# Four feature tiles share two passes of 64 + 64 inner rows in a feed-forward product, with other rules for the list scheduler

## The chip, the cores and the metric

One core of one Trainium2 chip runs the kernel. TensorE (PE) multiplies, VectorE (DVE) and ScalarE (ACT) do element work, GpSimd (POOL) and SyncE (SP) mostly issue transfers. The metric is the device time of one execution in microseconds (us). A weight load of PE (PEld) and a matmul are separate instructions of one engine.

## The reference

Two layers, each a windowed attention and a feed-forward part, over 2048 rows of 576 columns, all float32:

```python
    x = x + _A_ref(_layernorm(x, axis=-1), A_wqkv, A_wo)
    x = x + _B_ref(_layernorm(x, axis=-1), B_w1, B_w2)
    x = x + _A_ref(_layernorm(x, axis=-1), A_wqkv, A_wo)
    x = x + _B_ref(_layernorm(x, axis=-1), B_w1, B_w2)
```

`_A_ref` has 32 heads of 18 columns; a row attends to itself and the 7 rows that lie 2, 4, ... 14 before it. `_B_ref` is `silu(x @ w1) @ w2` with `w1` 576 x 4608 and `w2` 4608 x 576.

## The kernel before

**Tiling.** The rows are cut into four chunks of 512 (four tiles of 128 rows, index j). A stage s = 0 to 7 is one chunk of one layer: `front(s)` does attention, output projection and the layer norm ahead of the feed-forward part, `ffn(s)` the feed-forward part. The 4608 features are 36 tiles of 128, index f.

**Precision.** A float32 operand is split into a float16 high half and a float16 rest, the low half; a product is the sum of high x high, high x low and low x high. The inner dimension of 576 is four blocks of 128 and one of 64. Each full block takes three passes of a 128x128 weight tile against 512 columns. The block of 64 stands twice in the 128 partitions (high half of x in one, low half in the other), so that one pass gives two of its three parts; the third part (high x against the low half of the weights) needs only 64 partitions. So a feature tile takes 13 full passes and half a pass (`passes` yields 14; the last is the half one). `mm` issues the 13 passes of tile f, and `mm_both` the two half passes of the tiles f and f + 1: one on partitions 0 to 63, one on 64 to 127, into the two `z` banks. For this the transposed x (`xb`) carries a tenth section, which holds the block of 64 on the upper partitions.

**Down product.** `mm2` multiplies the activated tiles `h` with `w2` into `acc` (groups of 6 features in stage 0, of 9 later), `add_to` adds them to x. ACT applies silu (`hs <- z`) and makes the high half of `h`; DVE makes its low half.

**First chunk.** In stage 0 the weights come as float32 (`raw_load`, on POOL's queue), are scaled and split (`raw_split`: squares and high halves on ACT, low halves on DVE, L814 and L819) and are stored to DRAM for stages 1 to 7. In the same stretch DVE computes the attention of stage 1. PE also projects chunks 1 to 3 ahead of their attention (`qkv_ahead`).

**The order.** Every piece of work is an `op` with an engine, an assumed duration, a priority and what it reads and writes. `Plan.order` is a list scheduler: it simulates the engines with the assumed durations and issues, for each engine that is free, the ready op of the best priority whose buffers are free. What it returns is the fixed order of the program; each engine then works its own list in that order and waits for what is missing. The buffers matter here: `z` (2 PSUM banks), `misc` (2 banks, used by the projections and small sums), `acc` (2 x 2 banks), `h` (9), `hs` (3), `w1` (6), `w2` (11), `kv` (2).

**Transposes.** `transposed` turns the split layer norm with PE (`on_pe`) or with transposing DMAs on SP's queue.

Of the kernel before, what the change touches and what calls it, by code (L numbers as in the profile page):

```python
# [16 lines left out]
P = 128  # L17
# [7 lines left out]
NC = 4  # L25
NJ = 4
# [24 lines left out]
class Plan:  # L51
# [3 lines left out]
    LAT = 0.2  # L55
    DMA_IN, DMA_OUT = 1.2, 1.8
    DMA_RATE = 0.33e6

# [43 lines left out]
    def order(self):  # L102
        free = {t: list(range(len(x))) for t, x in self.tags.items()}
# [3 lines left out]
        ready = {e: [] for e in engines}  # L107
        events, out, tbl = [], [], None
        queues = {e: [] for e in engines}
# [57 lines left out]
        while done < len(self.ops):  # L167
# [12 lines left out]
            for e in engines:  # L180
# [7 lines left out]
                while ready[e]:  # L188
                    x = heapq.heappop(ready[e])
                    need = [b for b in x[2].bufs if b.slot is None]  # L190
                    n = {}
                    for b in need:
                        n[b.tag] = n.get(b.tag, 0) + 1
                    if all(len(free[t]) - want.get(t, 0) >= c for t, c in n.items()) and all(
                            self.turns[b.tag] in (None, b.turn) for b in need):
                        o = x[2]
                        break
                    for t, c in n.items():
                        want[t] = want.get(t, 0) + c
                    back.append(x)  # L200
# [11 lines left out]
                if e == "ACT" and o.table and o.table != tbl:  # L212
                    tbl = o.table
                    dur += 1.3
                o.start = now
                busy[e] = now + dur
# [15 lines left out]
def sliding_attention_silu_ffn(ctx: ExitStack, tc: tile.TileContext, x, wqkv, wo, w1, w2, out):  # L232
# [15 lines left out]
    def T(b):  # L248
        return S.tags[b.tag][b.slot]
# [24 lines left out]
    tag("acc", 2, [P, 2, 512], F32, ps, turns=False)  # L274
    tag("misc", 2, [P, 512], F32, ps, turns=False)

    xd = [[tc.dram_tile([P, D], F32, name=f"xd{c}{j}") for j in range(NJ)] for c in range(NC)]
# [55 lines left out]
    def passes(xk, wk):  # L333
# [6 lines left out]
        yield xk(4), wk(9)  # L340

    def halves_lo(src, f, s):
        for o, a, b in ((640, 0, 512), (D, 512, D)):
            nc.vector.scalar_tensor_tensor(f[:, o:o + b - a], src[:, a:b], s, f[:, a:b],  # L344
                                           op0=ALU.mult, op1=ALU.subtract)
# [24 lines left out]

    PE_LN = (1, 1, 1, 0)
    PACE_WQ, PACE_WO, PACE_W = (1, 7, 0, 6), (2, 2, 3, 3, 3), (4, 5, 6, 7)
# [231 lines left out]
    def attention(s, xT, wq, more=None):  # L604
# [4 lines left out]
        for u in range(NU):  # L609
# [11 lines left out]
            else:  # L621
# [13 lines left out]
                for j in range(NJ):  # L635
                    m = Buf("misc")

                    def evac(j=j, m=m, u=u, kv=kv, qt=qt):
                        d = du[:, u:u + 1]
                        nc.scalar.activation(T(kv)[:, j + W - 1].rearrange("p a b -> p (a b)"), T(m)[:, UC:3 * UC],  # L640
                                             AF.Copy, scale=d)
                        nc.scalar.activation(T(qt)[:, j, :], T(m)[:, 0:UC], AF.Copy, scale=d)
                    op("PE", 2.6, lambda j=j, m=m, w=w: qkv_matmul(xT, w, j, m),
                       [(xT, j)] + w.keys, [m], pr_)
                    op("ACT", 0.9, evac, [m, ("su", u)], [(kv, j), (qt, j)], pr_ - (0 if s else 9))
# [194 lines left out]
    def ffn(s, xT, xs):  # L840
# [3 lines left out]
        lay, c = divmod(s, NC)  # L844
        pair = {}
        for g in range(NFT // n):
# [8 lines left out]
            for f in range(g * n, (g + 1) * n):  # L855
                if f % 2 == 0:

                    for q in (f, f + 1):
                        wab = ws[q - g * n] if raw else (load_w1(q, pd), load_w2(q, pd))
                        pair[q] = (Buf("z"), *wab, *([[(w, 0), (w, 1)] for w in wab] if raw else [[w] for w in wab]))  # L860
                z, wa, wb, ka, kb = pair[f]
                hs, h = Buf("hs"), Buf("h")
                hb.append(h)
                wbs.append((wb, kb))

                def mm(z=z, wa=wa, f=f):
                    pl = list(passes(lambda k: T(xT)[:, k, :], lambda k: T(wa)[:, k, :]))[:-1]
                    for m, (u, v) in enumerate(pl):
                        nc.tensor.matmul(T(z), v, u, start=m == 0 and f % 2 == 0, stop=m == len(pl) - 1 and f % 2 == 1)  # L869

                def mm_both(f=f):
                    for q, p0, k in ((f, 0, 4), (f + 1, 64, 9)):
                        nc.tensor.matmul(T(pair[q][0]), T(pair[q][1])[p0:p0 + 64, 9, :], T(xT)[p0:p0 + 64, k, :],  # L873
                                         start=q != f, stop=q == f)
                xk = [(xT, j) for j in range(NJ)]
                op("PE", 2.81, mm, xk + ka, [z], pp)
                if f % 2 == 0:
                    op("PE", 0.3, mm_both, xk + ka + pair[f + 1][3], [z, pair[f + 1][0]], pp)
                op("ACT", 0.7, lambda z=z, hs=hs, f=f: nc.scalar.activation(T(hs), T(z), AF.Silu, scale=d1[:, f:f + 1]),  # L879
# [70 lines left out]
    def front(s):  # L950
# [22 lines left out]
        project(s, o, X[s])  # L973
        XT[s] = layer_norm(X[s], s - 1.0, "xb", s == 1, s == 0, True)

# [35 lines left out]
```

## Time and profile before

| what | value |
|---|---|
| median of 3 runs | 2227.76 us (2226.75 to 2228.0) |
| the profiled execution | 2227.76 us; span from first to last instruction 2226.0 us |
| PE busy | 2180.7 us (98%) |
| DVE busy | 1394.7 us (63%) |
| ACT busy | 758.1 us (34%) |
| mean granted clock of PE | 0.998 of 2.4 GHz |

The profiled execution's own time is its span plus 1.8 us around it, and is the median itself. Matmuls are pipelined: a matmul of 512 columns is listed with 380 ns, but the next one starts sooner, so what PE gets done is read from the starts of its instructions and not from their durations.

### The profile page before, as it was taken

The numbers are of one execution on the slowest core, as the hardware profiler recorded it, in microseconds if no ns is written. First come the engines' busy times: TensorE is split into PE (matmuls) and PEld (weight loads), VectorE is DVE, ScalarE is ACT, GpSimd is POOL, SyncE is SP. The second block draws the span as 40 slices with busy tenths as digits, with TensorE's granted clock in tenths as the row PEclk, the third lists the DMA queues.
The fourth block names the chain that finished last, engine by engine and source line by source line (L and its number), as shares of the span: only waits on it lengthen the run. The fifth ranks groups of instructions, "written<-read, shape, count | busy, mean of one in ns | idle before, by whom it ended". The sixth has DMA issues, their size and how long they took to land.

```text
span 2226.0 us, 33948 instructions
## 1 busy us (share of the span) xinstructions
PE 2180.7 (98%) x13862; PEld 1325.1 (60%) x13862; DVE 1394.7 (63%) x2047; ACT 758.1 (34%) x1219; POOL 205.1 (9%) x341
## 2 busy tenths in 40 slices
PE   5999999999999999999999999999999999999999
PEld 3556465656666666655666656656566566666665
DVE  7899989998988411249843598336873378621111
ACT  6456666643133122224212242222322223222222
POOL 2123454400001000000000000000000000000000
PEclk9999999999999999999999999999999999999999
DMA  5578666874555433445445454454445453353331
GB/s 162 155 203 277 229 230 208 258 214 158 145 186 161 113 107 103 149 128 176 115 119 157 131 151 122 126 159 140 130 116 136 149 162 114 70 140 121 114 111 42
DMA packets 225045, 333.11 MB, mean 150 GB/s; under 512 B 111720, under 2 KB 132052, under 8 KB 220920
## 3 DMA queue, kind: packets, MB, share of 16 engines
q1 hardware_dynamic: 195888, 231.39, 36.0%
q0 software_dynamic: 20704, 78.02, 10.4%
q10 hardware_dynamic: 8296, 21.52, 3.5%
q8 instruction: 108, 1.77, 0.3%
q14 instruction: 49, 0.40, 0.1%
HBM read 240.08 MB, written 47.03 MB: 129 GB/s over the span
## 4 chain that ended last, share of the span: by engine, by line
PE 90%; DMA 3%; DVE 3%; ACT 1%; issue 1%; POOL 1%; SPq 0%; ACTq 0%; DVEq 0%; POOLq 0%
PE acc L898 36%; PE z L869 34%; PE misc L573 9%; PE acc L743 4%; PE z L573 4%; PE z L873 2%; DMA w<-in_B_w_dram 1%; DMA h<-in_A_wqkv_dram 1%; DVE w L814 0%; DMA x<-in_A_x_dram 0%; DMA kv<-kd 0%; DVE pr L704 0%; DVE yh L344 0%; DMA kd<-hs 0%; DVE x L750 0%
## 5 line engine op out<-in xcount | busy, mean ns | idle before, releaser
L898 PE MATMUL acc<-w,h 128*128 128x288 f16 x6912 | 859.7, 286 | 2.3 <-DVE h L884 1.6
L869 PE MATMUL z<-xb,w 128*128 128x512 f16 x3744 | 841.5, 380 | 6.5 <-DVE w L814 6.3
L898 PEld LDWEIGHTS <-h 128*128 128x128 f16 x6912 | 675.7, 98 | 181.7 <-issue 4.0
L869 PEld LDWEIGHTS <-w 128*128 128x128 f16 x3744 | 355.7, 98 | 441.7 <-issue 31.4
L879 ACT ACTIVATE hs<-z,d 128x512 f32<-128x512 f32 x288 | 197.7, 686 | 1001.8 <-PE z L873 511.1
L884 DVE SCALAR_TENSOR_TENSOR h<-hs,sh,h 128x512 f16<-128x512 f32 x288 | 214.6, 749 | 391.0 <-ACT h L881 390.8
L750 DVE SCALAR_TENSOR_TENSOR x<-acc,d,x 128x576 f32<-128x576 f32 x135 | 110.1, 816 | 301.7 <-PE acc L898 301.6
L881 ACT ACTIVATE h<-hs,sh 128x512 f16<-128x512 f32 x288 | 207.4, 721 | 9.1
L573 PEld LDWEIGHTS <-xa 128*128 128x128 f16 x1344 | 131.9, 98 | 121.3 <-issue 7.2
L573 PE MATMUL misc<-wq,xa 128*128 128x432 f16 x1008 | 190.1, 349 | 3.6 <-ACT xa L360 2.5
L671 DVE TENSOR_TENSOR pr<-qt,kv 128x2304 f32<-128x2304 f32 x64 | 163.4, 2553 | 13.6 <-DMA kv<-kv 12.7
L704 DVE TENSOR_TENSOR pr<-kv,pe 128x1152 f32<-128x1152 f32 x128 | 169.2, 1352 | 1.1
L675 DVE TENSOR_REDUCE lg<-pr 128x128 f32<-128x2304 f32 x64 | 163.1, 2549 | 1.2
L711 DVE TENSOR_TENSOR pr<-pr 128x1152 f32<-128x1152 f32 (+1 forms) x128 | 135.3, 1057 | 3.6
L743 PE MATMUL acc<-wo,oT 128*128 128x288 f16 x896 | 113.5, 286 | 0.0
L743 PEld LDWEIGHTS <-oT 128*128 128x128 f16 x896 | 87.6, 98 | 22.7
L640 ACT ACTIVATE kv<-misc,du 128x288 f32<-128x288 f32 x80 | 40.0, 500 | 145.3 <-PE misc L573 98.1
L922 POOL DMA_DIRECT2D out_dram<-x x12 | 6.5, 544 | 685.6 <-DVE x L750 685.6
L573 PEld LDWEIGHTS <-xb 128*128 128x128 f16 x448 | 43.6, 98 | 39.1 <-ACT xb L360 1.9
L873 PE MATMUL z<-xb,w 64*128 64x512 f16 x288 | 57.3, 386 | 2.8 <-DMA x<-in_A_x_dram 2.6
L750 DVE SCALAR_TENSOR_TENSOR x<-acc,so,x 128x576 f32<-128x576 f32 x32 | 26.1, 816 | 48.1 <-PE acc L743 48.0
L390 DVE BATCH_NORM_STATS2 st<-x 128x6 f32<-128x288 f32 x128 | 51.8, 447 | 6.0 <-DMA x<-in_A_x_dram 4.8
(123 smaller groups left out, 1165.2 us busy)
## 6 DMA issues: line engine op xcount, KB each, us to landing
w<-w1s SPq DMA_DIRECT2D x252, 320.0 KB
w<-w2s SPq DMA_DIRECT2D x252, 288.0 KB
wq<-wqs SPq DMA_DIRECT2D x17, 1080.0 KB
kv<-kd POOLq DMA_DIRECT2D x8, 1584.0 KB, 8.6
w1s<-w POOLq DMA_DIRECT2D x36, 320.0 KB, 4.1
w<-in_B_w_dram POOLq DMA_DIRECT2D x36, 288.0 KB, 4.4
w2s<-w POOLq DMA_DIRECT2D x36, 288.0 KB, 4.0
kv<-kv ACTq DMA_DIRECT2D x20, 504.0 KB
```

Source lines behind the costliest of these rows:

```text
L573: nc.tensor.matmul(T(m)[:, :3 * UC], a, b, start=n == 0, stop=n == len(pl) - 1)
L671: nc.vector.tensor_tensor(T(pr), T(qt)[:, j:j + 2, None, :].to_broadcast([P, 2, W, UC]), win(T(kv), j, 2), op=ALU.mult)
L675: nc.vector.tensor_reduce(T(lg)[:, j:j + 2].rearrange("p a w h -> p (a w h)"), T(pr).rearrange("p a w (h d) -> p (a w h) d", d=DH), axis=A ...
L704: nc.vector.tensor_tensor(T(pr)[:, a].rearrange("p w (h d) -> p w h d", d=DH), v, T(pe)[:, j + a, :, :, None].to_broadcast([P, W, UH, DH]) ...
L711: nc.vector.tensor_tensor(t[:, :, 0:h, :], t[:, :, 0:h, :], t[:, :, h:2 * h, :], op=ALU.add)
L743: nc.tensor.matmul(T(acc)[:, h, 0:288], a, b[:, h * 288:(h + 1) * 288], start=n == 0, stop=n == len(pl) - 1)
L750: nc.vector.scalar_tensor_tensor(t, T(acc)[:, :, 0:288], d, t, op0=ALU.mult, op1=ALU.add)
L869: nc.tensor.matmul(T(z), v, u, start=m == 0 and f % 2 == 0, stop=m == len(pl) - 1 and f % 2 == 1)
L879: op("ACT", 0.7, lambda z=z, hs=hs, f=f: nc.scalar.activation(T(hs), T(z), AF.Silu, scale=d1[:, f:f + 1]), [z, ("s12", f)], [hs], pd, tabl ...
L881: op("ACT", 0.72, lambda hs=hs, h=h, f=f: nc.scalar.activation(T(h)[:, 0, :], T(hs), AF.Copy, scale=shs[i][:, f:f + 1]), [hs, ("sh", i, g) ...
L884: op("DVE", 0.75, lambda hs=hs, h=h, f=f: nc.vector.scalar_tensor_tensor(T(h)[:, 1, :], T(hs), shs[i][:, f:f + 1], T(h)[:, 0, :], op0=ALU. ...
L898: nc.tensor.matmul(T(acc)[:, h, 0:288], T(hb[q])[:, a, j * P:(j + 1) * P], T(wbs[q][0])[:, w, h * 288:(h + 1) * 288], start=q == 0 and m = ...
```

## The change

`block` replaces the pairing in stages 1 to 7. Four feature tiles form a block: the full passes of tiles 0 and 1 into the two `z` banks, then one `halves` op with four half passes (two for `z`, two that begin sums in the two `misc` banks), then the full passes of tiles 2 and 3 on top of these. A one-slot buffer `ticket` lets one block at a time stand between its first op and its `halves`. In stage 0 every tile takes 14 full passes and no half ones, and the transposed x has nine sections there. The layer norm of chunk 3 (fourth entry of `PE_LN`) is transposed by PE. The scheduler gets other constants for DMAs, a cost `MODE` for a change between full and half passes, another rule for which waiting op reserves buffers (one that lacks a single kind), and a rule that lets an op take several buffers of a kind that is handed out in turn. In layer two a projection writes a key of its `kv` buffer, so the buffer is taken when the projection is issued.

```diff
-    DMA_IN, DMA_OUT = 1.2, 1.8
-    DMA_RATE = 0.33e6
+    MODE = 0.1
+    DMA_IN, DMA_OUT = 1.2, 1.3
+    DMA_RATE = 0.29e6
...
-                            self.turns[b.tag] in (None, b.turn) for b in need):
+                            self.turns[b.tag] is None or b.turn - self.turns[b.tag] < n[b.tag] for b in need):
...
-                    for t, c in n.items():
-                        want[t] = want.get(t, 0) + c
+                    lacks = [t for t, c in n.items() if len(free[t]) - want.get(t, 0) < c]
+                    for t in lacks if len(lacks) == 1 else ():
+                        want[t] = want.get(t, 0) + n[t]
...
+                if e == "PE" and o.table != mode:
+                    mode = o.table
+                    dur += self.MODE
...
+    def block(items, dur, prio):
+        pl = [(a, b) for a, b in passes(lambda k: k, lambda k: k)][:-1]
+        tk = Buf("ticket")
+
+        def full(i):
+            def mm():
+                for m, (a, b) in enumerate(pl):
+                    u, v = items[i][2](a, b, slice(0, P))
+                    nc.tensor.matmul(items[i][0](), u, v, start=m == 0 and i < 2, stop=m == 12 and i > 1)
+            op("PE", dur * 13, mm, items[i][1] + ([tk] if i == 0 else []), [items[i][3]], prio)
+
+        def halves():
+            for i, p0, k in ((0, 0, 4), (1, 64, 9), (2, 0, 4), (3, 64, 9)):
+                u, v = items[i][2](k, 9, slice(p0, p0 + 64))
+                nc.tensor.matmul(items[i][0](), u, v, start=i > 1, stop=i < 2)
+        full(0)
+        full(1)
+
+        op("PE", dur * 2, halves, sum((x[1] for x in items), [tk]), [x[3] for x in items], prio, table="halves")
+        full(2)
+        full(3)
...
-    PE_LN = (1, 1, 1, 0)
+    PE_LN = (1, 1, 1, 1)
...
-                       [(xT, j)] + w.keys, [m], pr_)
+                       [(xT, j)] + w.keys, [m] + [(kv, "hold", j)] * (s >= NC), pr_)
...
+                if raw:
+                    z, (wa, wb) = Buf("z"), ws[f - g * n]
...
+                            nc.tensor.matmul(T(z), v, u, start=m == 0, stop=m == len(pl) - 1)
+                    op("PE", 3.03, mm, xk + [(wa, 0), (wa, 1)], [z], pp)
+                else:
+                    if f % 4 == 0:
+                        four = [(Buf(("z", "z", "misc", "misc")[q - f]), load_w1(q, pd), load_w2(q, pd))
+                                for q in range(f, f + 4)]
...
-        XT[s] = layer_norm(X[s], s - 1.0, "xb", s == 1, s == 0, True)
+        XT[s] = layer_norm(X[s], s - 1.0, "xb", s == 1, s == 0, s > 0)
```

**PE, at a half pass of stages 1 to 7.** Before, PE's list reads as follows where the tiles in the banks `z_133` and `z_132` share a pass (`w` is the weight tile, `xb` the transposed x, L869 a full and L873 a half pass):

```order
L869 MATMUL z_133<-xb_75,w_101 128x512
L873 LDWEIGHTS w_101
L873 MATMUL z_133<-xb_75,w_101 128x512
L873 LDWEIGHTS w_100
L873 MATMUL z_132<-xb_75,w_100 128x512
L869 LDWEIGHTS w_100
```

In the changed program the same place of a block reads as follows (L359 is a full pass, L365 a half one):

```order
L359 MATMUL z_133<-xb_76,w_99 128x512
L365 LDWEIGHTS w_97
L365 MATMUL z_132<-xb_76,w_97 128x512
L365 LDWEIGHTS w_99
L365 MATMUL z_133<-xb_76,w_99 128x512
L365 LDWEIGHTS w_100
L365 MATMUL misc_136<-xb_76,w_100 128x512
L365 LDWEIGHTS w_102
L365 MATMUL misc_137<-xb_76,w_102 128x512
L359 LDWEIGHTS w_100
```

Four half passes now follow each other, and the third and the fourth load weights into the partitions that the first and the second use.

**DVE, at the end of the first chunk.** These are the low halves of the last features of stage 0 (`h_118`, `h_119`), as DVE's list has them before; L704, L711 and L712 are the second product of an attention unit and its sum over the window, L344 is the layer norm's low half:

```order
L884 SCALAR_TENSOR_TENSOR h_118<-hs_124,sh_279,h_118 128x512
L344 SCALAR_TENSOR_TENSOR yh_93<-y_91,nt_131,yh_93 128x512
L344 SCALAR_TENSOR_TENSOR yh_93<-y_91,nt_131,yh_93 128x64
L704 TENSOR_TENSOR pr_87<-kv_79,pe_85 128x1152
L884 SCALAR_TENSOR_TENSOR h_119<-hs_125,sh_279,h_119 128x512
L711 TENSOR_TENSOR pr_87<-pr_87 128x2x576
```

In the changed program the same features stand among the first products and sums of the attention unit behind it (L702 and L706, which are L671 and L675 before; L913 is L884):

```order
L913 SCALAR_TENSOR_TENSOR h_116<-hs_124,sh_279,h_116 128x512
L702 TENSOR_TENSOR pr_87<-qt_82,kv_80 128x2304
L913 SCALAR_TENSOR_TENSOR h_117<-hs_125,sh_279,h_117 128x512
L913 SCALAR_TENSOR_TENSOR h_118<-hs_123,sh_279,h_118 128x512
L706 TENSOR_REDUCE lg_84<-pr_87 128x128
L913 SCALAR_TENSOR_TENSOR h_119<-hs_124,sh_279,h_119 128x512
```

Counted from the start of DVE's list, the last low half of stage 0 (the 36th L884) has the same work ahead of it as before and in addition one L671, one L675, two L704, two long and two short L711, two L712 and two pairs of L344 (of 512 and of 64 columns).

## Rows read from the trace of the kernel before

**Rows 1.** Stretches: length, busy us of each engine, PE's clock, DMA share, GB/s.

```profile
222.70:475.40 252.70, 238.69 (x1527) 146.37 (x1525) 230.08 (x362) 162.25 (x282) 110.12 (x193) 0.99 0.72 226
475.40:2226.00 1750.60, 1746.60 (x11130) 1066.40 (x11129) 970.02 (x1314) 469.98 (x699) 37.46 (x58) 1.00 0.45 132
```

**Rows 2.** Waits of PE, 20 to 500 us, then from 500 on: total, times, longest.

```profile
PE z L869 <- DVE w L814: 6.3, 4, 1.8
PE z L873 <- DMA x<-in_A_x_dram: 2.6, 1, 2.6
...
PE acc L898 <- DVE x L908: 0.6, 1, 0.6
```

**Rows 3.** Timeline of PE, 330 to 640 us: start us, us, line, xcount.

```profile
451.60 17.80 PE L898 MATMUL acc<-w,h 128*128 128x288 f16 x144
...
533.44 0.39 PE L873 MATMUL z<-xb,w 64*128 64x512 f16 x2
533.76 5.79 PE L869 MATMUL z<-xb,w 128*128 128x512 f16 x26
539.48 0.39 PE L873 MATMUL z<-xb,w 64*128 64x512 f16 x2
...
551.88 2.98 PE L869 MATMUL z<-xb,w 128*128 128x512 f16 x13
554.69 17.80 PE L898 MATMUL acc<-w,h 128*128 128x288 f16 x144
```

**Rows 4.** Timeline of PE's weight loads at the same place.

```profile
533.43 0.10 PEld L873 LDWEIGHTS <-w 64*128 64x128 f16 x2 [0.42 <-issue]
533.75 5.29 PEld L869 LDWEIGHTS <-w 128*128 128x128 f16 x26 [0.23 <-issue]
```

**Rows 5.** Timeline of PE at transposes of the layer norm.

```profile
216.10 1.28 PE L358 MATMUL acc<-ident,yh 128*128 128x128 f16 x20
217.21 2.72 PE L573 MATMUL z<-wq,xa 128*128 128x432 f16 x14
```

**Rows 6.** Groups of DVE by shape, 0 to 500 us: count, busy us, mean ns.

```profile
L671 DVE TENSOR_TENSOR pr<-qt,kv 128x2304 f32<-128x2304 f32 x21 | 53.6, 2552 | 0.4
L704 DVE TENSOR_TENSOR pr<-kv,pe 128x1152 f32<-128x1152 f32 x40 | 53.2, 1353 | 0.4
L675 DVE TENSOR_REDUCE lg<-pr 128x128 f32<-128x2304 f32 x20 | 51.0, 2548 | 0.3
...
L711 DVE TENSOR_TENSOR pr<-pr 128x1152 f32<-128x1152 f32 x20 | 27.1, 1356 | 0.4
...
L711 DVE TENSOR_TENSOR pr<-pr 128x576 f32<-128x576 f32 x20 | 15.2, 758 | 0.7
L344 DVE SCALAR_TENSOR_TENSOR yh<-y,nt,yh 128x512 f16<-128x512 f32 x14 | 10.5, 747 | 4.5 <-ACT yh L440 4.5
L712 DVE TENSOR_TENSOR o<-pr 128x288 f32<-128x288 f32 x20 | 9.2, 458 | 1.0
```

**Rows 7.** Timeline of DVE at the last low half of stage 0.

```profile
454.19 0.75 DVE L884 SCALAR_TENSOR_TENSOR h<-hs,sh,h 128x512 f16<-128x512 f32 x1
```

**Rows 8.** Waits of DVE, 187 to 436 us.

```profile
DVE x L750 <- PE acc L898: 6.4, 8, 2.4
DVE h L884 <- ACT h L881: 3.8, 2, 1.9
DVE w L814 <- ACT w L812: 2.0, 2, 1.6
DVE w L819 <- ACT w L817: 2.0, 2, 1.6
```

**Rows 9.** Timeline of PE at the start of stage 1.

```profile
475.11 0.37 PE L873 MATMUL z<-xb,w 64*128 64x512 f16 x1 [2.58 <-DMA x<-in_A_x_dram]
475.41 7.47 PE L869 MATMUL z<-xb,w 128*128 128x512 f16 x26
```

**Rows 10.** A stretch behind that wait; columns as in group 1.

```profile
476.40:479.70 3.30, 3.30 (x10) 1.13 (x8) 3.27 (x4) 0.00 (x0) 0.00 (x0) 0.50 1.04 399
```

More of the change, by code (lines that the diff above doesn't have):

```diff
@@ L107, in order @@
         ready = {e: [] for e in engines}
-        events, out, tbl = [], [], None
+        events, out, tbl, mode = [], [], None, None
         queues = {e: [] for e in engines}
@@ L275, in sliding_attention_silu_ffn @@
     tag("misc", 2, [P, 512], F32, ps, turns=False)
+    S.slots("ticket", [None], False)
     xd = [[tc.dram_tile([P, D], F32, name=f"xd{c}{j}") for j in range(NJ)] for c in range(NC)]
@@ L844, in ffn @@
         lay, c = divmod(s, NC)
-        pair = {}
+        xk = [(xT, j) for j in range(NJ)]
         for g in range(NFT // n):
@@ L855, in ffn, with mm @@
             for f in range(g * n, (g + 1) * n):
[L856 to L861, printed above, removed]
+                if raw:
+                    z, (wa, wb) = Buf("z"), ws[f - g * n]
+                    kb = [(wb, 0), (wb, 1)]
+                    def mm(z=z, wa=wa):
+                        pl = list(passes(lambda k: T(xT)[:, k, :], lambda k: T(wa)[:, k, :]))
+                        for m, (u, v) in enumerate(pl):
+                            nc.tensor.matmul(T(z), v, u, start=m == 0, stop=m == len(pl) - 1)
[4 more added lines that the diff above has]
+                                for q in range(f, f + 4)]
+                        block([(lambda z=z: T(z), xk + [wa],
+                                lambda k, q, r, wa=wa: (T(wa)[r, q, :], T(xT)[r, k, :]), z)
+                               for z, wa, wb in four], 0.217, pp)
+                    z, wa, wb = four[f % 4]
+                    kb = [wb]
                 hs, h = Buf("hs"), Buf("h")
@@ L864, in ffn @@
                 wbs.append((wb, kb))
[L866 to L878, printed above, removed]
                 op("ACT", 0.7, lambda z=z, hs=hs, f=f: nc.scalar.activation(T(hs), T(z), AF.Silu, scale=d1[:, f:f + 1]),
```

## The prediction

> **What bounds the kernel now.** I first cut the span in two where the last long wait of PE ends. From 475.4 us to the end PE is busy 1746.6 of 1750.6 us, while DVE has 970.0 and ACT 470.0; between 222.7 and 475.4 us PE has 238.7 and DVE 230.1 of 252.7 [rows 1]. So four fifths of the time are PE's alone, and ahead of that lies a stretch in which two engines are nearly full. The waits of PE say the same: between 20 and 500 us it waits for the low halves of raw weights that DVE makes (6.3 us) and once for the transposed x of stage 1 (2.6 us); after 500 us it waits 0.6 us in all [rows 2]. In the long part only less PE work can save time, and it saves all that it takes away. In the first part the question is what DVE has ready when.
>
> The busy times don't tell what a matmul costs, so I went to the timeline. Thirteen full passes of 512 columns start at 551.88 and the next op at 554.69: 0.216 us each. A pair of half passes starts at 533.44, full passes follow at 533.76, and the next pair stands at 539.48, 6.04 us after the first [rows 3]. The 26 full passes between are 5.62 us, so a pair of half passes takes 0.42 us in PE's list, where one pass at the full rate would take 0.216: changing to half passes and back costs 0.20 us, about half on each side (0.32 - 0.216 behind, 5.72 - 5.62 ahead). The weight loads show why: they stop 0.42 us ahead of the pair and 0.23 us behind it, whereas in full passes 26 loads lie within the 5.72 us of the matmuls [rows 3, 4].
>
> **The change part by part.**
>
> *Half passes, stages 1 to 7.* Before there are 18 pairs in each of seven stages, 126 changes there and back. Now there are 9 blocks in each, 63. The passes stay the same in number (126 pairs before; 63 times two pairs now). What goes is 63 x 0.20 = 12.6 us, if the second pair of a block starts one full pass behind the first. All of these come at or after 472 us, where PE is the bound, so nothing hides them and nothing hides their saving. No row of before has two half passes behind each other on the same partitions, so the price of the second pair is bounded: at least 0.216 us (its columns), at most 0.32 us (what follows a pair now), or 0.42 with a whole change. I take 0.216, since a weight load lasts 0.10 us and is hidden behind matmuls of its own partitions in every full pass [rows 3, 4]; the upper ends stay for the range.
>
> *First chunk.* 36 tiles take 14 full passes: for two tiles 28 x 0.216 = 6.05 us against 6.04, nothing. The tenth section of the transposed x goes there (4 transposes less on PE), and 36 transposes of chunk 3 come to PE from SP's queue. Twenty take 217.21 - 216.10 = 1.11 us [rows 5], so 32 more are 1.8 us of PE, with four evacuations on ACT, which is busy 162 of 252.7 us in the stretch behind [rows 1]. They lie ahead of 222 us. Their cover is PE's waiting for DVE later on; without that they cost 1.8 us.
>
> *The new order of DVE.* DVE's instructions are the same, their order is not. Attention of stage 1 and 2 moves forward, the low halves of weights and of h move back. PE's order in the first chunk hardly changes: its work ahead of the same places is about 2 us more. The place that decides is the last low half of stage 0, since the last group's down product and everything of stage 1 stand behind it. By the order it has one L671, one L675, two L704, two long and two short L711, two L712 and two L344 more ahead of it: 2.55 + 2.55 + 2.71 + 2.71 + 1.52 + 0.92 + 1.49 = 14.5 us [rows 6]; the two short L344 have no row and are left out. Other places are like it: the 21st low half of w1 has two L671, two L675, a long and a short L711 and an L712 more ahead of it, 12.8 us. These are not added; the later place contains them.
>
> Before, this half ends at 454.9 [rows 7], and PE needs it at the thirty-first matmul of the product that starts at 451.60: 451.60 + 30 x 17.80/144 = 455.3 [rows 3]. The slack is 0.4 us, so PE gets there up to 14.5 - 0.4 = 14.1 us later. Two things are set against that. First, DVE itself waits before: in the four largest groups 14.2 us between 187 and 436 us [rows 8]. The two longest (6.4 us for a down product, 3.8 us for ACT's high half) are those of instructions that stand later in DVE's list now, while what they wait for on PE stands 2 us later; they should go, and some new waits come with the attention that moved forward. I call what is saved S, between 0 and 14 us, and take 8. Second, the transposed x of stage 1 is begun earlier, since the last L344 of its layer norm has some 10 us less DVE work ahead of it. Before, PE waits 2.58 us for it and then works 26 passes in 7.47 us instead of 5.79 [rows 3, 9]; the granted clock there is 0.50, the lower level of 1.2 GHz, after that wait [rows 10]. These 2.6 + 1.7 = 4.3 us should fall away, being behind a DVE that is late anyway. What the first part costs is then 14.1 - 4.3 - S = 9.8 - S: between +9.8 and -4.4 us, and +1.8 with S = 8.
>
> *The rest.* The list of reservations, the turns, the ticket and the `kv` key act through the order alone. In stages 1 to 7 PE's list has the blocks, projections and down products in an order with two full tiles (5.6 us) between the moment a bank of `misc` gets its last pass and the moment the next block needs it; I cost it at nothing, and treat its failure below.
>
> **Sum.** The profiled execution took 2227.8 us, the median itself (its span is 2226.0). 2227.8 - 12.6 + 1.8 = 2217.0.
>
> **The rivals.**
>
> *Half passes don't hide their weights.* The third half pass loads into the partitions in which the first still works. If it waits until these are through, as the first full pass behind a pair does now, the second pair costs 0.10 us more, 63 x 0.10 = 6.5 us, and the time is 2223.5; with a whole change for it nothing is saved and the time is 2229.6. For it speaks the stop of 0.23 us behind a pair; against it, that there the kind of pass changes, and that loads of 128 rows run behind matmuls on the same 128 rows [rows 4]. The Trainium skill has the rule that would bring this about: in "TensorE: Matmul & The Clock Gate", Part 3, "The mechanism", a weight load overlaps a running matmul only where its row group is another one. By that rule the gain would be about half; this case's full passes disagree with it, and no row shows half passes. Chance 0.10.
>
> *Slower: DVE is later still.* If DVE, in the first chunk, waits more than before instead of less, S is negative, and each us of it delays the last low half of stage 0 by one. The raw weights and their high halves come through POOL's queue and ACT, both worked strictly in order, and the moved attention can stand in DVE's list ahead of its inputs. From S = -2.8 (17.0 us instead of 14.2 in those four groups) the change loses what it gains; from S = -7.3 on the time is over 2232.2. Against it speaks that the longest of these waits lose their cause. Chance 0.06, at about 2231.
>
> *The block waits for its banks.* `halves` needs four banks at once, and a block ends in `misc` banks that projections of layer two also use. A wait of 0.2 us in each block eats all: 63 x 0.2, 2229.6. Against it stand the 5.6 us of full passes between, and that PE waits 0.6 us in all after 500 us now [rows 2]. Chance 0.05.
>
> *The first part gains.* If DVE loses nearly all of its waits, S is 14 or over and the time is 2210.8 or below. Chance 0.09.
>
> **How the numbers follow.** My forecast, the remaining 0.70, is 2217 with a range of its own from 2211 (S = 14) to 2225 (S = 0). A measurement here tells about 0.2% from no change, 2223.3 to 2232.2. Below lie most of the forecast (0.65; S over 1.7), the last rival (0.09), half of the first rival (0.05) and a part of the third (0.02): 0.81. Between lie 0.05 of the forecast, 0.05 of the first, 0.03 of the third and 0.02 of the second rival: 0.15. Above lies 0.04. The range is 2209 to 2225: it leaves out the rivals that lose the whole gain, and the far end of the last one.
>
> **What would show it.** Right: in stages 1 to 7 four half passes whose third starts 0.216 us after the first, full passes 0.32 us after the third, and PE work per stage shorter by 1.8 us. Wrong: a third half pass 0.3 us behind or later; waits of PE at `halves` in layer two. For the first part: L814 and h waits of PE in the first chunk longer than 6.3 us, the transposed x of stage 1 no longer waited for, DVE's waits in 187 to 436 us shorter by S, and the first full pass of the second block of stage 1 within some 2 us of where it stands before. The prediction is wrong if PE's idle time ahead of stage 1 grows by over 8 us or shrinks by over 6, or if the pair in the block isn't hidden.

## The result, and the profile after

The changed kernel takes 2237.05 us (median of 5 runs, 2232.64 to 2239.84) against 2227.06 us for the kernel before on the same chip: a ratio of 1.0043, with a 95% interval of 1.0029 to 1.0058. It is slower by 0.4%, where 2217.0 us was forecast. The profiled execution took 2236.56 us, its span is 2234.8 us, 8.8 us more than before.

In the code after, L359 is a full and L365 a half pass, L894 a pass of stage 0, L927 the down product and L781 its addition to x, L908 silu, L910 and L913 the high and low half of `h`, L702 and L706 the first attention product and its sum, L671 and L673 the evacuation of a projection (ACT's copies out of PSUM), L683 the halo copies (transfers inside `kv` that bring each partition the earlier rows of its windows), L774 the output projection, L845 the low half of a raw weight (L898, L750, L879, L881, L884, L671, L675, L640, L642, L652, L743 and L814 before).

I read the same cuts as before. The stretches of [rows 1] come out as follows in the changed kernel (length, busy us of PE, PEld, DVE, ACT and POOL, PE's clock, DMA share, GB/s):

```profile
222.70:475.40 252.70, 236.47 (x1474) 145.68 (x1473) 230.25 (x363) 164.25 (x286) 108.99 (x191) 0.97 0.72 222
475.40:2235.00 1759.60, 1742.45 (x11187) 1073.10 (x11184) 966.32 (x1310) 445.87 (x686) 38.55 (x60) 1.00 0.45 132
```

In the long part PE is busy 4.2 us less than before, but idle 17.2 us instead of 4.0. That is no longer the part in which PE never waits. The waits of PE, from 20 to 500 us and then from 500 us on (total, times, longest), answer [rows 2]:

```profile
PE z L894 <- ACT hs L908: 9.6, 7, 2.2
PE acc L774 <- DMA oT<-yh: 4.4, 2, 2.2
...
PE z L894 <- DVE w L845: 2.2, 3, 1.0
...
PE acc L927 <- DVE x L781: 12.3, 4, 3.7
PE acc L927 <- DVE x L937: 0.6, 1, 0.6
```

Four waits of a down product for DVE's addition, 12.3 us, are new. There was none after 500 us but the last one of 0.6 us, which is still there.

**The half passes did what was forecast.** The timeline of PE in stage 3 of the changed kernel (start, us, line) answers [rows 3]:

```profile
931.93 5.78 PE L359 MATMUL z<-xb,w 128*128 128x512 f16 x26
937.64 0.39 PE L365 MATMUL z<-xb,w 64*128 64x512 f16 x2
937.87 0.38 PE L365 MATMUL misc<-xb,w 64*128 64x512 f16 x2
938.18 5.79 PE L359 MATMUL misc<-xb,w 128*128 128x512 f16 x26
943.80 5.78 PE L359 MATMUL z<-xb,w 128*128 128x512 f16 x26
```

The second pair starts 0.23 us behind the first (0.226 where the trace gives nanoseconds), the full passes 0.31 us behind the second. From one block's first full pass to the next block's it is 943.80 - 931.93 = 11.87 us; two pairs and their full passes took 2 x 6.04 = 12.08. That is 0.21 us a block and 13 us for 63. The weight loads answer [rows 4]:

```profile
937.64 0.11 PEld L365 LDWEIGHTS <-w 64*128 64x128 f16 x4 [0.42 <-issue]
938.17 9.83 PEld L359 LDWEIGHTS <-w 128*128 128x128 f16 x47 [0.42 <-issue]
```

They stop on both sides of the four half passes, where the kind of pass changes, and not inside.

**Where the time went.** The chain of the first new wait, at about 1005 us, runs through three engines. PE's timeline in the changed kernel (in brackets how long it was idle before, and what ended that):

```profile
958.47 20.60 PE L604 MATMUL misc<-wq,xa 128*128 128x432 f16 x112
978.91 2.97 PE L359 MATMUL z<-xb,w 128*128 128x512 f16 x13
981.82 0.39 PE L365 MATMUL z<-xb,w 64*128 64x512 f16 x2
...
987.97 13.39 PE L927 MATMUL acc<-w,h 128*128 128x288 f16 x108
1005.09 7.10 PE L927 MATMUL acc<-w,h 128*128 128x288 f16 x43 [3.73 <-DVE x L781]
```

ACT in the same stretch (ACTq rows are transfers that ACT issues):

```profile
974.53 2.92 ACTq L683 DMA_DIRECT2D kv<-kv  x4
977.50 0.50 ACT L671 ACTIVATE kv<-misc,du 128x288 f32<-128x288 f32 x1 [2.72 <-PE misc L604]
...
979.51 0.37 ACT L673 ACTIVATE qt<-misc,du 128x144 f32<-128x144 f32 x1
979.64 12.11 ACTq L683 DMA_DIRECT2D kv<-kv  x4
991.86 0.69 ACT L908 ACTIVATE hs<-z,d 128x512 f32<-128x512 f32 x1 [11.97 <-DMA kv<-kv]
992.57 0.72 ACT L910 ACTIVATE h<-hs,sh 128x512 f16<-128x512 f32 x1
```

And DVE:

```profile
993.33 0.75 DVE L913 SCALAR_TENSOR_TENSOR h<-hs,sh,h 128x512 f16<-128x512 f32 x1 [32.77 <-ACT h L910]
994.00 2.55 DVE L702 TENSOR_TENSOR pr<-qt,kv 128x2304 f32<-128x2304 f32 x1
...
1001.76 2.55 DVE L706 TENSOR_REDUCE lg<-pr 128x128 f32<-128x2304 f32 x1
1004.23 0.81 DVE L781 SCALAR_TENSOR_TENSOR x<-acc,d,x 128x576 f32<-128x576 f32 x1
```

Read together, the three timelines say this. A block puts two full tiles ahead of its half passes, so the tiles in `z` are finished together, here at 982 us, behind a projection of two units (20.6 us). ACT has evacuated the projection by then and its list goes on with the second unit's halo copies. The issue of these four copies takes 12.11 us, that of the first four 2.92. The silu, whose input was finished at 982, starts at 991.86. DVE has been waiting 32.77 us for its product; then its list has four attention instructions of together 10.2 us, and the addition that frees `acc` behind them. PE needs that bank of `acc` at 1001.36, and gets it 3.73 us late. Before, the pair's `mm_both` stood straight behind the projection, and the silu ahead of the same copies. ACT's timeline of the kernel before:

```profile
978.70 0.69 ACT L879 ACTIVATE hs<-z,d 128x512 f32<-128x512 f32 x1
979.42 0.72 ACT L881 ACTIVATE h<-hs,sh 128x512 f16<-128x512 f32 x1
979.43 4.17 ACTq L652 DMA_DIRECT2D kv<-kv  x4
```

The same happens once at each front of a stage of layer two. PE runs at the lower clock after the first and the last of the four waits, and at the full one after the other two. Windows of the changed kernel: the 12.11 us of the copies, the stretch behind the first wait, and that behind the last:

```profile
979.64:991.75 12.11, 12.11 (x72) 6.49 (x71) 0.00 (x0) 0.24 (x1) 0.53 (x1) 1.00 1.02 296
...
1006.00:1009.40 3.40, 3.40 (x16) 2.17 (x15) 3.26 (x7) 0.42 (x1) 0.00 (x0) 0.50 0.00 0
1818.40:1821.80 3.40, 3.40 (x16) 2.16 (x15) 2.85 (x6) 0.42 (x1) 0.00 (x0) 0.50 0.02 5
```

A granted clock of 0.50 is the lower of the two levels, 1.2 GHz; 3.4 us at it cost 1.7 us, twice. Layer two so loses 12.3 + 3.4 = 15.7 us. With the 13 us gained, 8.8 + 13 - 15.7 leaves +6.1 us for the first part; this is a remainder and was not read from its rows.

**The first part.** DVE's last low half of stage 0, which ended at 454.9 [rows 7], ends at 465.7:

```profile
465.00 0.74 DVE L913 SCALAR_TENSOR_TENSOR h<-hs,sh,h 128x512 f16<-128x512 f32 x1
```

DVE's waits from 187 to 436 us (answer to [rows 8]) are others, but not less: 15.3 us in the four largest groups against 14.2.

```profile
DVE yh L375 <- ACT yh L759: 5.0, 2, 4.2
DVE x L781 <- PE acc L927: 4.3, 5, 1.3
DVE p L335 <- PE misc L834: 3.6, 1, 3.6
DVE w L845 <- ACT w L843: 2.4, 3, 1.9
```

PE's wait for the transposed x of stage 1 [rows 9] is gone, and with it the half clock behind it [rows 10]. But the clock between 222.7 and 475.4 us is 0.97 instead of 0.99, and PE is idle there 16.2 us instead of 14.0.

That late low half is not what PE waits for. PE's timeline at the end of stage 0, first in the kernel before, then in the changed one:

```profile
448.78 2.98 PE L869 MATMUL z<-xb,w 128*128 128x512 f16 x13
```

```profile
458.33 3.18 PE L894 MATMUL z<-xb,w 128*128 128x512 f16 x14 [0.71 <-ACT hs L908]
461.35 4.57 PE L927 MATMUL acc<-w,h 128*128 128x288 f16 x36
...
468.79 13.39 PE L927 MATMUL acc<-w,h 128*128 128x288 f16 x108
```

Before, PE was through with the last tile of stage 0 at 451.60; now it is at 461.35, 9.75 us later, and so late already before the half is made. It never waits for a low half of `h` between 222.7 and 475.4 us. Its longest waits there are for a bank of `z` that ACT's silu still reads (9.6 us in seven waits, first of the rows that answer [rows 2]), where before they were for the low halves of raw weights (6.3 us then, 2.2 now). Two of those silu waited for a low half on DVE themselves (2.5 us together); the others stood behind ACT's other work, mostly on raw weights. Four stretches of 3.4 us have a clock of 0.51 to 0.61, behind two such waits (from 313.2 and 358.2 us) and behind two for the transposed attention output `oT` (from 395.2 and 402.6); before there is one, of 0.54 from 370.8.

### The profile page after: what moved, and what is told of

It reads as the page before. It is cut to its first block, busy times and chain, and to the rows that moved or that the text cites. A ratio compares the mean times of both kernels' runs of the same rounds, so it can differ in the third digit from the quotient of the medians.

```text
span 2234.8 us, 34093 instructions
## 1 busy us (share of the span) xinstructions
PE 2175.2 (97%) x13894; PEld 1332.1 (60%) x13894; DVE 1394.0 (62%) x2047; ACT 739.0 (33%) x1211; POOL 203.9 (9%) x341
## 4 chain that ended last, share of the span: by engine, by line
PE 86%; DVE 6%; DMA 5%; ACT 2%; issue 1%; POOL 0%; ACTq 0%; SPq 0%; DVEq 0%
PE acc L927 35%; PE z L359 16%; PE misc L359 15%; PE misc L604 8%; PE acc L774 4%; PE z L604 4%; PE z L894 2%; DMA kv<-kv 1%; DVE lg L706 1%; DVE pr L702 1%; DMA w<-w1s 1%; PE z L365 1%; DMA oT<-yh 1%; PE misc L365 1%; DMA h<-in_A_wqkv_dram 1%
## 5 line engine op out<-in xcount | busy, mean ns | idle before, releaser
L927 PE MATMUL acc<-w,h 128*128 128x288 f16 x6912 | 861.9, 287 | 13.0 <-DVE x L781 12.3
L927 PEld LDWEIGHTS <-h 128*128 128x128 f16 x6912 | 677.9, 98 | 192.7 <-issue 13.9
L359 PEld LDWEIGHTS <-w 128*128 128x128 f16 x3276 | 315.3, 98 | 392.5 <-issue 26.3
L913 DVE SCALAR_TENSOR_TENSOR h<-hs,sh,h 128x512 f16<-128x512 f32 x288 | 211.1, 748 | 379.3 <-ACT h L910 379.1
L359 PE MATMUL z<-xb,w 128*128 128x512 f16 x1638 | 364.8, 379 | 0.0
L359 PE MATMUL misc<-xb,w 128*128 128x512 f16 x1638 | 364.4, 379 | 0.0
L910 ACT ACTIVATE h<-hs,sh 128x512 f16<-128x512 f32 x288 | 206.9, 721 | 397.5 <-PE acc L927 389.7
L781 DVE SCALAR_TENSOR_TENSOR x<-acc,d,x 128x576 f32<-128x576 f32 x135 | 109.9, 814 | 298.8 <-PE acc L927 298.7
L908 ACT ACTIVATE hs<-z,d 128x512 f32<-128x512 f32 x162 | 109.7, 678 | 536.0 <-PE z L365 471.5
L702 DVE TENSOR_TENSOR pr<-qt,kv 128x2304 f32<-128x2304 f32 x64 | 163.4, 2553 | 1.1
L706 DVE TENSOR_REDUCE lg<-pr 128x128 f32<-128x2304 f32 x64 | 163.1, 2549 | 1.4
L894 PE MATMUL z<-xb,w 128*128 128x512 f16 x504 | 116.0, 387 | 11.7 <-ACT hs L908 9.6
L774 PE MATMUL acc<-wo,oT 128*128 128x288 f16 x896 | 117.9, 291 | 4.4 <-DMA oT<-yh 4.4
L908 ACT ACTIVATE hs<-misc,d 128x512 f32<-128x512 f32 x126 | 86.0, 686 | 107.3 <-PE misc L359 103.4
L774 PEld LDWEIGHTS <-oT 128*128 128x128 f16 x896 | 88.9, 99 | 30.8 <-DMA oT<-yh 5.2
L894 PEld LDWEIGHTS <-w 128*128 128x128 f16 x504 | 50.0, 100 | 72.7 <-DVE h L913 6.6
L671 ACT ACTIVATE kv<-misc,du 128x288 f32<-128x288 f32 x80 | 40.0, 500 | 154.1 <-PE misc L604 147.4
```

The source lines that it names most:

```text
L359: nc.tensor.matmul(items[i][0](), u, v, start=m == 0 and i < 2, stop=m == 12 and i > 1)
L702: nc.vector.tensor_tensor(T(pr), T(qt)[:, j:j + 2, None, :].to_broadcast([P, 2, W, UC]), win(T(kv), j, 2), op=ALU.mult)
L706: nc.vector.tensor_reduce(T(lg)[:, j:j + 2].rearrange("p a w h -> p (a w h)"), T(pr).rearrange("p a w (h d) -> p (a w h) d", d=DH), axis=A ...
L774: nc.tensor.matmul(T(acc)[:, h, 0:288], a, b[:, h * 288:(h + 1) * 288], start=n == 0, stop=n == len(pl) - 1)
L894: nc.tensor.matmul(T(z), v, u, start=m == 0, stop=m == len(pl) - 1)
L910: op("ACT", 0.72, lambda hs=hs, h=h, f=f: nc.scalar.activation(T(h)[:, 0, :], T(hs), AF.Copy, scale=shs[i][:, f:f + 1]), [hs, ("sh", i, g) ...
```

## The experiments

Theory A: layer two loses its time because a silu stands behind halo copies in ACT's list. Theory B: the addition is late because it stands behind attention in DVE's list, whatever ACT does. The first part's loss is a separate matter. Ratios are to the kernel before on the same chip, with their 95% interval.

**1. The halo copies of layer two on POOL's queue** (the planner still counts them on ACT, so the order of the rest is the same):

```diff
-    nc.scalar.dma_start(t[p0 + d:p0 + d + n, i:i + m], t[p0:p0 + n, 11 - m:11])
+    (nc.scalar if s < NC else nc.gpsimd).dma_start(t[p0 + d:p0 + d + n, i:i + m], t[p0:p0 + n, 11 - m:11])
```

> The changed kernel with one edit: in layer two the four copies of each halo are issued by POOL and no longer by ACT; the plan, and with it the order on PE, DVE, SP and of ACT's other work, is that of the changed kernel. Theory A (ACT's queue): the four waits of PE for an add of DVE at 1005, 1277, 1547 and 1818 us (12.3 us) arise because the silu of a block stands behind the second halo in ACT's list, and that halo's last copy is issued only when a weight load has landed; then they go, with the half-clock stretches behind the first and the last (3.4 us): about 2237 - 15.7 = 2221 us. Theory B (DVE's list): the add stands behind 10 us of attention products, and is late whatever ACT does: the four waits stay and the time stays at 2237 us.

Measured: 2219.43 us, ratio 0.9964 (0.9951 to 0.9977), 17.6 us less than the changed kernel. In its trace the silu starts at 981.65, and the down product takes 216 matmuls at a stretch. PE's timeline there:

```profile
981.23 0.39 PE L365 MATMUL z<-xb,w 64*128 64x512 f16 x2
...
987.39 26.62 PE L927 MATMUL acc<-w,h 128*128 128x288 f16 x216
```

All four waits are gone with DVE's list as it was, so theory B is refuted. By the span (2217.9) the first part still costs 2217.9 - 2226.0 + 13 = 4.9 us.

**2. All of the change but the blocks** (stages 1 to 7 with pairs as before; `...` stands for lines left out):

```diff
-    block([(lambda z=z: T(z), xk + [wa],
...
-           for z, wa, wb in four], 0.217, pp)
...
+    op("PE", 2.82, mm, xk + [wa], [z], pp)
+    if f % 2 == 0:
+        op("PE", 0.217, mm_both, xk + [wa, pair[f + 1][1]], [z, pair[f + 1][0]], pp, table="halves")
```

> The changed kernel without the blocks: stages 1 to 7 take the pairs of before, everything else (first chunk, scheduler constants, list of reservations, kv key, PE transposes) stays. In its ACT list the silu of the pair stands ahead of the second halo again. Theory A: the four waits go, the saving of the blocks (63 x 0.206 = 13.0 us) goes too, and what is left over the kernel before is the first 500 us (1.8 us of transposes, 1.3 us more idle, two more half-clock stretches 3.4 us): 2227 + 6.5, about 2233.5 us. Theory B: waits of the same size in layer two stay: about 2237 + 13 = 2250 us, or 2246 without the half-clock stretches.

Measured: 2232.95 us, ratio 1.0023 (1.0014 to 1.0033), 5.3 us slower than before. PE waits 0.6 us after 500 us. Windows of this version:

```profile
222.70:475.40 252.70, 234.59 (x1467) 144.45 (x1466) 229.85 (x364) 164.25 (x287) 108.44 (x190) 0.98 0.73 221
475.40:2233.90 1758.50, 1753.84 (x11203) 1072.82 (x11200) 969.49 (x1313) 470.50 (x699) 39.02 (x61) 1.00 0.47 132
```

So the four long waits need the blocks, and the first part loses about 5 us without them.

**3 and 4. The blocks alone, and all of the change without the `kv` key.** The first is the kernel before with `block`, `ticket`, `MODE` and the rule on turns that it needs; in the second the projections of layer two do not take their `kv` buffer at issue:

```diff
-    [(xT, j)] + w.keys, [m] + [(kv, "hold", j)] * (s >= NC), pr_)
+    [(xT, j)] + w.keys, [m], pr_)
```

> The kernel before with the blocks alone in stages 1 to 7 (with the ticket, the cost for a change of pass and the rule that lets an op take several buffers in turn); first chunk, DMA constants, list of reservations, transposes and kv key as before. In its ACT list all four halos of a chunk of layer two stand ahead of the silu of the block that is under way. If the loss of the first 500 us belongs to the other edits, the stretch up to 475 us is like that of before. Theory A: silu is held back behind four halos and the attention ahead of them in each of four stages, so PE waits in layer two at least as long as in the changed kernel (12 us) and perhaps tens of us: 2227 - 13 + 12 or more, 2226 to 2290 us. Theory B (DVE's order, not ACT's): the waits are not tied to the halos and can be small: about 2214 us.

> The changed kernel without the key that takes a kv buffer when the projection is issued. ACT's list then has all four halos of a chunk of layer two ahead of the silu of the block under way, as with the blocks alone; the first chunk is that of the changed kernel. Theory A: the same long waits in layer two as with the blocks alone, and the first 500 us of the changed kernel on top: the time of the blocks alone plus about 6.5 us. Theory B: waits of some 12 us as in the changed kernel: about 2237 us.

Measured: 2327.31 us, ratio 1.0451 (1.0437 to 1.0464), and 2337.28 us, ratio 1.0493 (1.0479 to 1.0506). The first is above all that was expected of it (2226 to 2290 us), and the place is another than the one in the changed kernel, so these two runs say little on theory A. PE's waits after 500 us in the version with the blocks alone:

```profile
PE misc L603 <- ACT qt L672: 100.8, 8, 15.3
```

ACT's timeline at one of them, in the same version:

```profile
998.37 0.50 ACT L670 ACTIVATE kv<-misc,du 128x288 f32<-128x288 f32 x1 [9.57 <-DVE pr L734]
```

PE projects a third unit while both `kv` buffers are still read by DVE. ACT cannot evacuate, the two banks of `misc` stay full, and PE stands still for 12.6 us on average, twice in each stage of layer two. The key keeps such a projection out of PE's list until a buffer is free. So with blocks the key is worth about 100 us.

**5 to 8. What costs in the first part.** Each is experiment 1 with something of the first part put back: stage 0 with pairs and ten sections of the transposed x; chunk 3 turned by SP's queue; the old constants for DMAs; all three together. The cut is shortened, and the remarks behind # are not in the code.

```diff
-    op("PE", 3.03, mm, xk + [(wa, 0), (wa, 1)], [z], pp)              # 5 and 8: 14 passes a tile
+    op("PE", 2.81, mm, xk + ka, [z], pp)                              # 13, and a pair of half passes for two
+    op("PE", 0.3, mm_both, xk + ka + [(wn, 0), (wn, 1)], [z, pair[f + 1][0]], pp)
-    PE_LN = (1, 1, 1, 1)                                              # 6 and 8
+    PE_LN = (1, 1, 1, 0)
-    DMA_IN, DMA_OUT = 1.2, 1.3                                        # 7 and 8
-    DMA_RATE = 0.29e6
+    DMA_IN, DMA_OUT = 1.2, 1.8
+    DMA_RATE = 0.33e6
```

> The changed kernel with the halo copies on POOL's queue (2219.4 us, 4.9 us more in the first part than before, by 2217.9 - 2226.0 + 13.0), and stage 0 as before: 13 full passes a tile and a pair of half passes for two tiles, ten sections of the transposed x. If the 14 passes of stage 0 and the order around them make the loss of the first part (theory P), it goes back to about 2214.5. If it is the transposes of chunk 3 on PE (theory T), the constants for DMAs (theory C) or the list of reservations (theory L), it stays at 2219.4 within 1.5 us.

> The changed kernel with the halo copies on POOL's queue, and the layer norm of chunk 3 transposed by SP's queue as before (PE_LN 1, 1, 1, 0). Theory T: the 1.8 us of PE and what their four evacuations and banks hold up go away, about 2214.5 to 2217.5. Theories P, C and L: 2219.4 within 1.5 us; if only the 1.8 us of transposes count, 2217.6.

> The changed kernel with the halo copies on POOL's queue, and the planner's old constants for DMAs (1.8 us out, 0.33e6 instead of 1.3 and 0.29e6), which act on the order alone. Theory C: 2214.5. Theories P, T and L: 2219.4 within 1.5 us.

> The three together: blocks, new list of reservations, turns, ticket and kv key, halo copies on POOL's queue; stage 0, PE_LN and the DMA constants as before. If the loss of the first part is made by any of P, T or C or by several of them, 2214.5 (2227.5 less the 13.0 us of the half passes). If it is the list of reservations (L), 2219.4 within 1.5 us. In layer two no wait of PE for DVE over 1 us by either.

Measured, beside a kernel before of 2228.58 us:

| version | us | ratio (95%) |
|---|---|---|
| 5, stage 0 with pairs | 2209.07 | 0.9915 (0.9901 to 0.9928) |
| 6, chunk 3 by SP | 2220.30 | 0.9961 (0.9948 to 0.9973) |
| 7, old DMA constants | 2219.57 | 0.9958 (0.9946 to 0.9971) |
| 8, all three | 2212.05 | 0.9922 (0.9908 to 0.9935) |

It is stage 0 (theory P; what of it, experiment 12 asks). The transposes of chunk 3 and the constants are worth nothing by themselves. Version 5 is even below the 2214.5 us that it would take if only the loss went. Its first part (window 222.7 to 475.4) has PE idle 9.2 us, against 19.8 in experiment 1 and 16.2 in the changed kernel. Experiment 1, then version 5:

```profile
222.70:475.40 252.70, 232.95 (x1484) 144.90 (x1483) 231.59 (x364) 164.79 (x287) 108.99 (x191) 0.99 0.73 222
222.70:475.40 252.70, 243.54 (x1542) 148.42 (x1539) 231.65 (x363) 163.42 (x286) 110.14 (x193) 0.99 0.75 230
```

The waits for the silu fall from 8.9 us in experiment 1 to 2.5 in version 5. That they alone set the time of the first part is not shown: in the profile of version 7 they are 1.5 us, but one wait of 6.3 us for the transposed x of stage 1 stands there instead.

**9. The order alone, with the copies on ACT.** The changed kernel, in whose finished list the second unit's four copies stand behind the next two silu instead of ahead of them (shortened):

```diff
+    if s >= NC and u % 2:
+        halos.append(hal)
...
-    for o in S.order():
+    L = S.order()
+    for o in halos:
+        i = L.index(o)
+        act = [k for k in range(i + 1, len(L)) if L[k].eng == "ACT"]
+        if L[act[0]].table == "silu" and L[act[2]].table == "silu":
+            L.insert(act[2], L.pop(i))
+    for o in L:
```

> The changed kernel with one place of ACT's list altered in each stage of layer two: the four halo copies of the second unit stand behind the next two silu, still on ACT's queue. Theory A (what costs is that a silu stands behind copies whose issue waits): the four waits of PE for DVE's addition (12.3 us and 3.4 us of half clock) go, about 2221 us. Rival A2 (what costs is that ACT's queue issues copies at all in this place, since the issue holds up whatever stands behind it): the waits return at the other two silu or the exponential, over 2230. Rival A3 (the wait is for the bank or for DVE, the queue only seems to be late): 2237, no change.

Measured: 2221.89 us, ratio 0.9969 (0.9958 to 0.9981). ACT's timeline there:

```profile
986.95 0.69 ACT L910 ACTIVATE hs<-z,d 128x512 f32<-128x512 f32 x1 [2.35 <-PE z L365]
987.67 0.72 ACT L912 ACTIVATE h<-hs,sh 128x512 f16<-128x512 f32 x1
987.76 0.53 ACTq L683 DMA_DIRECT2D kv<-kv  x1
988.29 0.67 ACT L910 ACTIVATE hs<-z,d 128x512 f32<-128x512 f32 x1
988.33 3.03 ACTq L683 DMA_DIRECT2D kv<-kv  x3
```

The copies are still ACT's, 8 us later, and their issue takes 0.53 + 3.03 = 3.6 us instead of 12.11. PE does not wait. So it is the place in the list that costs, with the long issue that comes with it there, and not the queue as such.

**10. The kernel before with the copies on POOL's queue** (the edit of experiment 1 alone).

> The kernel before, with the halo copies of layer two on POOL's queue and nothing else. Theory A: there the silu stands ahead of these copies, so nothing is won; 2227.7 within 1.5 us. If POOL's queue is simply the better one for these copies, so that the 17.6 us between the changed kernel and its version with POOL are not of the new order, 2220 or less.

Measured: 2226.72 us, ratio 0.9994 (0.9985 to 1.0002). POOL's queue is no better for these copies where no silu stands behind them.

**11. The changed kernel with stage 0 in pairs,** the copies on ACT (the first edit of 5 without that of 1).

> The changed kernel with stage 0 as before (pairs of half passes, ten sections) and nothing else, the halo copies on ACT's queue again. If the two losses are independent, 2237.0 less the 10.4 us between 2219.4 and 2209.1, 2226.7. If the one hides the other, outside 2223 to 2230.

Measured: 2226.37 us, ratio 0.9995 (0.9985 to 1.0005). The two losses add up. PE's waits there hold the four of layer two almost unchanged:

```profile
PE acc L937 <- DVE x L781: 12.1, 4, 3.6
```

**12. Another order of stage 0 with the same instructions.** Experiment 1, with another assumed duration of a tile in the planner:

```diff
-    op("PE", 3.03, mm, xk + [(wa, 0), (wa, 1)], [z], pp)
+    op("PE", 2.96, mm, xk + [(wa, 0), (wa, 1)], [z], pp)
```

> The changed kernel with the halo copies on POOL's queue, and 2.96 instead of 3.03 us as the planner's assumed duration of a feature tile in stage 0: the same instructions (14 full passes a tile), another order in the first part alone. Theory P1 (the 10 us come from the order that the planner happens to find, not from 14 passes as such): the time moves by over 2 us from 2219.4, to either side. Theory P2 (from the passes or the wait for both banks in each tile): 2219.4 within 1.5 us.

Measured: 2213.37 us, ratio 0.9935 (0.9922 to 0.9948), 6.1 us less than experiment 1. Its window of the first part:

```profile
222.70:475.40 252.70, 239.04 (x1540) 149.65 (x1538) 238.13 (x371) 163.98 (x287) 110.08 (x193) 1.00 0.75 233
```

PE is idle 13.7 us there (19.8 in experiment 1), and the clock stays at 1.00. So another order of the same instructions, 14 passes a tile included, wins 6 of the 10 us between experiments 1 and 5. The other 4 us remain between 14 passes and pairs, or their orders; no run takes these apart.

## Why the prediction was wrong

- **Half passes: right.** Forecast -12.6 us, measured -13 (0.21 us x 63). The rival that they don't hide their weights is refuted: the third starts 0.226 us behind the first, not 0.3 or 0.4. The rule that I had set against this, in the Trainium skill under "TensorE: Matmul & The Clock Gate", Part 3, "The mechanism" (a weight load overlaps only where the row group differs), disagrees with this trace: the third and the fourth load go into the 64 rows in which the first and the second pass work, and all four loads are listed within 0.11 us (at 937.64), while these two passes have just begun.
- **"The rest": the step that failed.** It said that reservations, turns, ticket and key act through the order alone, and "I cost it at nothing", because of two full tiles between the last pass into a bank of `misc` and its next use. That was an argument on banks, and they indeed hold: PE doesn't wait at `halves`, and the third rival is refuted. What I didn't follow is who else stands in the lists. A block finishes its first tile 13 passes later than a pair did, so the silu moved behind the halo copies in ACT's list, and DVE's addition behind four attention instructions. The prediction followed the lists through the first chunk and not at the fronts of layer two, where the four waits and their half clock cost 15.7 us by the trace and 17.6 us by experiment 1. Experiments 9 and 10 show that it is this order.
- **The slack that I read off was not there.** PE's 0.6 us of waiting after 500 us [rows 2] told me that nothing in that part was tight. It tells only that nothing was late. In the kernel before, the four copies stood straight behind the silu in ACT's list; the margin was one place in a list, and no view of waits shows that.
- **First part: the sign right, the size and the path not.** Forecast 9.8 - S = +1.8 with S = 8; it costs 5.3 us in experiment 2, and 6.1 as the remainder above, within the bounds of +9.8 and -4.4. The late low half came, 10.8 us later than before (14.5 - S with S = 3.7), and 10.8 - 0.4 - 4.3 is again 6.1. But that agreement is luck: PE did not wait for this half; it was 9.75 us late by itself, and its longest waits were for ACT's silu, which the prediction did not have. The sign that it named, waits for raw weights and `h` of over 6.3 us, did not come (2.2 us). How much of the 9.75 us the order of DVE makes, by way of the silu, stays open. DVE did not lose its waits either, which by themselves would make S -1.1: of the two that I expected to go, that for ACT's high half fell from 3.8 to 0.4 us, that for a down product only from 6.4 to 4.3, and others came. The 4.3 us at the start of stage 1 were won, as forecast. Experiment 12 shows that the order alone moves this part by 6 us.
- **The rival on the slower side** had the right sign in the wrong place: it put the loss into the first chunk, and all that lies above was given a chance of 0.04.

The sum of the profiled execution is -13 + 15.7 and the remainder of 6.1, +8.8 us. Since the last term is what was left, this checks nothing; the experiments do, which give the parts apart: -13 + 17.6 for the copies + 5.3 for the first part is 9.9 us, and the medians differ by 10.0.

## What to carry to other kernels

When a change makes two results finish together that finished one after the other, look up what stands behind the first of them in every engine's list: an engine that is a third busy can still be late, if its list has something slow ahead of what the bottleneck needs. Work that stands behind a transfer in the list of the engine that issues it waits until the issue is over, so compare the planner's 3.2 us for the four copies with the trace's 2.9 to 12.1. And where a list scheduler makes the order, a change of one assumed duration by 0.07 us moved this kernel by 6 us: judge an edit with its order held, or with several orders. Here the edit that pays is the blocks and the `kv` key, with the copies out of ACT's queue and stage 0 left in pairs: with the rest of the change as it is, 2209.07 us (experiment 5), 0.85% faster than before.

## What the runs showed of the hardware

**The issue of a copy can hold its engine for 12 us.** The same four copies of a halo take ACT's queue 2.92 us at 974.53 for one unit and 12.11 us at 979.64 for the next, in which time the DMA share is 1.02 of 16 engines, and ACT, idle otherwise, cannot start the silu behind them. The Trainium skill says in "DMA: Bandwidth & Descriptors", "Issuing engines are not separate DMA queues", that issuing from several engines saves only the time of the sequencer that initiates the transfer, which is usually small next to the transfer itself. Experiment 10 agrees that nothing else is saved (0.9994), but the 12.11 us were not small for what stood behind: moving four copies a unit was worth 17.6 us where that was a silu. A full DMA alone does not explain the 12.11 us: in experiment 9 the same four take 3.6 us at a share of 0.99. What the slow issues wait for stays open.

**Changing between full and half passes** costs about 0.1 us on each side, with four half passes between as with two: 0.31 us from the second pair to the full passes in a block, 0.32 behind a single pair before, where full passes follow each other at 0.216.
